# Five tiles' output stores move from ScalarE's queue to SP's, with a new written-out order for tiles 3 to 8

## The chip, the cores and the metric

The kernel runs on one core of one Trainium2 chip. The metric is the device time of one execution in microseconds (us), the median of several runs. The core has a matrix engine (TensorE, PE in the profile, with its weight loads listed as PEld), three engines for elementwise work (VectorE = DVE, ScalarE = ACT, GpSimd = POOL) and SyncE (SP), which does nothing here but start transfers. Each engine works through its own list of instructions in order and waits on semaphores where an instruction needs what another engine makes. A transfer is started by an instruction in the list of one engine (ACT, SP or POOL); "ACTq" and "SPq" in the profile are such starts.

## The reference

```python
q, k, v: [8 batches, 8 heads, 576, 64] float32
scores = (q @ k.T) / 8                  # per batch and head
scores = where(block_i >= block_j, scores, -1e9)   # blocks of 64 positions
attn   = softmax(scores) @ v
x      = attn.transpose(0, 2, 1, 3).reshape(4608, 512)
out    = (relu(x @ w_gate) * (x @ w_val)) @ w_out  # [512,1536], [512,1536], [1536,512]
```

`out` is [4608, 512] in float32.

## The kernel before

**Tiles.** The feed-forward part is worked in nine tiles of 512 rows of x. Tile j below 8 holds the first 512 positions of batch j; tile 8 holds the last 64 positions of all eight batches. While TensorE does the feed-forward of tile j, it also does the attention of batch j+1, and the inputs of batch j+2 are loaded. Tile 7 therefore carries no attention, and tile 8 none either.

**Order.** Nothing is left to a scheduler: from `with tc.manual_schedule` on, the instructions of all engines are issued in the order in which strings of tokens say. `ORDER_0` covers tiles 0 to 2. Tiles 3 to 6 all run `ORDER_3_6`, then come `ORDER_7` and `ORDER_8`; `program(j)` turns each token into instructions. As the order of the string is the order in every engine's list, moving a token moves its place on its own engine. `*n` after a token means n steps of it.

**The two matrix products of a tile.** Most pairs of 128 hidden features are made by a Strassen-like scheme with seven products in place of eight. For feature pair N the tokens are:
- `pN1` to `pN7`: the seven products, two steps each, and two matmuls of 128 x 256 columns into PSUM per step (`times`, L1363). They need sums of weights (`U..`, L979) and sums of x (`X4` to `X7`; `Y..` for tile 8; L1171).
- `pNa`, `pNu`, `pNw`: ScalarE copies a PSUM bank to an SBUF buffer (L1385). After that TensorE may write the bank again.
- `pNd`, `pNe`, `pNc`: VectorE adds a bank to such a buffer (L1389).
- `pNr`: relu on ScalarE (L1334); `pNH` and `pNL`: gate times value, giving half of a hidden tile hT (L1401, and L1405 with the relu included). `pNL` is on VectorE, `pNH` on VectorE or POOL.
- `gF`, `vF`, `rF`, `hF`: the same for one feature block without the scheme (L1339). Tiles 7 and 8 have none of these.

The product with w_out is done in the same way: `s....` are sums of hT (L1020), `M1` to `M7` the seven products, six steps of two matmuls each (L1061); `oa`, `ou`, `ow`, `oy` are ScalarE copies (L1106), `od`, `oe`, `oc` VectorE sums (L1100). In tile 8 `oy` is split into `oya` (ScalarE) and `oyb` (VectorE, L1118), `oc` into `oca` and `ocb`.

**Stores.** Each tile has four stores of 256 KB: `S2`, `S1`, `S0`, and the fourth, `S3`, which is put off into the next tile, where its token is `P`. They are issued in `put_block` (L893) for tiles 3 to 7: from ScalarE's queue, and for tile 2 from SP's. Tile 8's stores (`Sa`, `Sb`, `S2`, `Sya`, `S1`, `Syb`, two transfers each, L906) are spread over SP, ACT and POOL.

**Attention.** `Ai` makes the scores of head pair i of the next batch (L631), `Ei.` their exponentials on ScalarE (L636, L643), `Ci.` clears the masked corners (VectorE L1516 or POOL L1519), `Vi.` multiplies with v (L779), `Ni.` divides (L718), and `Ti` sends the result transposed into x by a transfer on SP (L862). `K` and `k` do the last 64 keys. `l0` to `l10` load q and k and `w0` to `w5` load v, started by POOL (L509); `d0` to `d3` transpose q and k by transfers on SP (L519 to L526).

**Where things go.** `ON_POOL` names the sums, products and clears that run on POOL, all others of their kind run on VectorE. `SLOTS` lists which of the rotating buffers each request takes (`sc` two and `ffnp` three PSUM buffers, `ob` five SBUF buffers of 128 x 512 float32, `gate_sb` three). `PAIR_BANK`, `OUT_BANK` and `AV_BANK` say which of the PSUM pools (`sc`, `one`, `ffn`) a product goes to.

Of the kernel before, what the change touches and what calls it, by code (L numbers as in the profile page):

```python
# [17 lines left out]
def kernel(  # L18
# [91 lines left out]
    ORDER_8 = """  # L110
        p01 p31 p01 p0a p17 p11*2 p1a X4 p07 p17 p07 p0w p06 p12 p06 p0u p12 p1c p16*2
        p04 p05*2 p0d p21 p1u p15*2 p31 p1w p1d p14*2 p1e p3a p04 p1L p0e p21 p2a p03*2
        p0r p0H p13 p02 p13 p1r p02 p0c P p1H p36 p26*2 p2u p27*2 p2w p41 p32 p25 p32
        p41 p4a p25 s0002 p0L s0102 p2d p3c p37*2 p3w p36 p3u p24*2 p2e p23*2 p2r p2H
        p34*2 p3e p35 p47 p35 p3d p22*2 p47 p2c p4w p3L p2L p42 p51*2 p5a p42 p33*2 p3r
        p3H p4c p46*2 p56 p44*2 p4u p4e p4L p56 p5u p57*2 p5w p45*2 p4d p55*2 p5d p54*2
        p5e M2 p52 p43 p52 p5c p5L p53 p43 p4r p4H p53 p5r p5H M1*2 M2 M1*4 M2*4 s0202
        s1002 s1202 oa s2002 s2202 M6*2 M7 s2102 M6*4 s1102 M7 s0302 s2302 M7*4 ou oca
        Sa M5*5 ocb s1302 Sb ow M5 od M4 S2 M4*3 M3*3 oya Sya M4*2 oe S1 M3*3 oyb Syb
# [38 lines left out]
        (7, 2): ('ffn', 'ffn', 'ffn'),
        (7, 3): ('one', 'ffn', 'sc'),
        (7, 4): ('ffn', 'one', 'ffn'),  # L160
        (7, 5): ('sc', 'sc', 'ffn'),
# [1655 lines left out]
```

## Time and profile before

| | |
|---|---|
| time, median of 3 runs | 344.81 us (344.55 to 344.91) |
| the profiled execution's own time | 344.71 us |
| its span | 342.8 us |
| mean granted TensorE clock | 0.997 |
| TensorE busy (matmuls) | 332.7 us, 97% |
| VectorE / ScalarE / POOL busy | 233.1 / 210.8 / 216.7 us |
| tile 3, tile 4, tile 5, tile 6 (start of one to start of the next) | 35.70, 35.62, 35.61, 34.83 us |
| tile 7; tile 8 to the end of the span | 28.00; 33.20 us |
| stores from ScalarE (L893 and earlier lines) | 28 transfers of 256 KB |

All times of instructions are from the profiled execution and count from the start of its span; times between runs are compared with the median. Copies, sums and products count as busy; starting a transfer does not, so ACTq and SPq rows stand apart from ACT's and SP's busy time. `[0.58 <-DVE hT L1405]` behind a row means that the engine was idle for 0.58 us before it and that an instruction of VectorE of line L1405 ended the wait. Matmuls are pipelined: a matmul of 256 columns starts 0.109 us after the one before when nothing is missing, though the row of one alone is longer.

### The profile page before, as it was taken

To read this page: it belongs to the slowest core of one execution; us is meant where nothing else is said; L and a number is where in the kernel's file an instruction comes from. 1 tells how busy PE (TensorE), PEld (TensorE's weight loads), DVE (VectorE), ACT (ScalarE), POOL (GpSimd) and SP (SyncE) were. 2 spreads that over 40 slices of the span, in tenths; PEclk is the share of its full clock that TensorE was granted. 3 is DMA by queue.
4 is the path that set the end of the run, shared out by engine and by line. 5 is a ranking of instruction groups with operands and counts; after the bars stand their busy time and mean duration, and the time that the engine had idled before them with its cause. 6 is when DMAs were issued, how large, how long until landed. Compare 5 with 4: busy or idle time off the path is not lost.

```text
span 342.8 us, 8917 instructions
## 1 busy us (share of the span) xinstructions
PE 332.7 (97%) x3477; PEld 233.8 (68%) x3518; DVE 233.1 (68%) x540; ACT 210.8 (61%) x344; POOL 216.7 (63%) x272
## 2 busy tenths in 40 slices
PE   8899999999999999999999999999999999999994
PEld 4544455545545558777877787777777788888883
DVE  4854445668637887389538972898279958966992
ACT  4942757588325882778558764876488727637731
POOL 2766566488695912787778967986514694750631
PEclk9999999999999999999999999999999999999998
DMA  8999999999998999799899989996510140002004
GB/s 242 294 351 371 368 230 238 240 163 155 187 197 137 144 158 137 165 143 121 111 165 120 130 116 153 128 137 118 138 33 2 33 122 12 2 31 94 33 0 122
DMA packets 155337, 50.06 MB, mean 146 GB/s; under 512 B 134496, under 2 KB 151648, under 8 KB 155296
## 3 DMA queue, kind: packets, MB, share of 16 engines
q0 software_dynamic: 70576, 9.12, 43.6%
q1 hardware_dynamic: 77536, 32.52, 43.0%
q10 hardware_dynamic: 7184, 7.87, 7.8%
q8 instruction: 27, 0.44, 0.5%
q14 instruction: 14, 0.11, 0.1%
HBM read 37.75 MB, written 9.44 MB: 138 GB/s over the span
## 4 chain that ended last, share of the span: by engine, by line
PE 88%; issue 4%; DVE 2%; ACT 2%; POOL 2%; POOLq 0%; DVEq 0%; ACTq 0%
PE ffnp L1179 16%; PE ffnp L1363 9%; PE ffnp L1339 8%; PE sc L1363 8%; PE sc L1061 6%; PE ffnp L1282 6%; PE ffnp L1061 6%; PE one L1363 5%; PE one L1061 4%; PE sc L631 3%; PE one L631 2%; PE one L779 2%; PE ffnp L779 2%; PE one L1179 2%; PE sc L779 1%
## 5 line engine op out<-in xcount | busy, mean ns | idle before, releaser
L636 ACT ACTIVATE attnT<-sc 128x1024 bf16<-128x1024 f32 x56 | 56.7, 1036 | 0.0
L1189 ACT ACTIVATE gate_sb<-ffnp 128x512 bf16<-128x512 f32 x35 | 20.6, 599 | 27.3 <-PE ffnp L1179 24.4
L1179 PE MATMUL ffnp<-xT,wg 128*128 128x512 bf16 x130 | 36.2, 379 | 0.6
L1061 PEld LDWEIGHTS <-stage 128*128 128x128 bf16 x336 | 32.0, 98 | 4.1 <-issue 0.2
L1363 PEld LDWEIGHTS <-stage 128*128 128x128 bf16 x288 | 27.3, 98 | 7.8
L779 PEld LDWEIGHTS <-attnT 128*128 128x128 bf16 x640 | 26.3, 98 | 7.7 <-DVE xnat L718 1.2
L1179 PE MATMUL ffnp<-xT,wv 128*128 128x512 bf16 x108 | 31.3, 380 | 0.2
L1199 DVE TENSOR_TENSOR hT<-gate_sb,ffnp 128x512 bf16<-128x512 bf16 x28 | 19.2, 684 | 14.9 <-PE ffnp L1179 12.0
L1389 DVE TENSOR_TENSOR ob<-ffnp,ob 128x512 f32<-128x512 f32 x29 | 19.8, 684 | 12.6 <-ACT ob L1385 12.6
L509 POOL DMA_DIRECT2D v_bf<-in_v_dram x30 | 24.3, 829 | 6.0 <-PE sc L793 3.1
L1061 PEld LDWEIGHTS <-hT 128*128 128x128 bf16 x252 | 24.2, 98 | 5.3 <-DVE hT L1405 1.1
L1363 PEld LDWEIGHTS <-wg 128*128 128x128 bf16 x224 | 21.9, 98 | 5.1
L1363 PEld LDWEIGHTS <-wv 128*128 128x128 bf16 x224 | 21.5, 98 | 5.3 <-ACT attnT L636 1.1
L1106 ACT COPY ob<-sc 128x512 f32<-128x512 f32 x13 | 7.6, 586 | 28.4 <-PE sc L1061 27.0
L1519 POOL MEMSET attnT<- 64x256 bf16 x34 | 10.2, 314 | 23.4 <-ACT attnT L636 16.0
L1282 PE MATMUL ffnp<-wo,hT 128*128 128x512 bf16 x91 | 23.1, 379 | 0.2
L1179 PEld LDWEIGHTS <-wg 128*128 128x128 bf16 x144 | 13.3, 98 | 13.8 <-issue 0.5
L1179 PEld LDWEIGHTS <-wv 128*128 128x128 bf16 x144 | 13.0, 98 | 14.3 <-issue 1.5
L1334 ACT ACTIVATE gate_sb<-ffnp 128x512 bf16<-128x512 f32 x30 | 17.6, 603 | 8.1 <-PE ffnp L1363 4.6
L509 POOL DMA_DIRECT2D q_bf<-in_q_dram x20 | 18.0, 908 | 5.0 <-DVE recip L752 4.0
L643 ACT ACTIVATE attnT<-one 128x512 bf16<-128x512 f32 (+1 forms) x28 | 15.0, 537 | 9.8 <-PE ffnp L631 8.4
L1020 POOL TENSOR_TENSOR stage<-hT,stage 128x512 bf16<-128x512 bf16 x15 | 17.4, 1167 | 4.2 <-DVE stage L1020 3.6
(228 smaller groups left out, 918.3 us busy)
## 6 DMA issues: line engine op xcount, KB each, us to landing
...
```

What stands on the lines that cost most here:

```text
L509: ins = nc.gpsimd.dma_start(dst, part_of)
L636: return lambda: nc.scalar.activation(at[:, :, lo : lo + 512], sc, AF.Exp, scale=scale)
L779: nc.tensor.matmul(av[:, p, :], at[:, col : col + 128], v_bf[b % 2][:, c, h, :], start=(p == 0), stop=(c == p), skip_group_check=True,)
L1061: nc.tensor.matmul(to, sums.of(c)[which][:, 128 * p : 128 * p + 128], right, start=first, stop=(c == 5), skip_group_check=True,)
L1179: nc.tensor.matmul(to, (wg, wv)[t][f // 4][:, c, 128 * (f % 4) : 128 * (f % 4) + 128], x[:, c], start=(c == 0), stop=(c == 3),)
L1189: nc.scalar.activation(gate_sb, gate, AF.Relu)
L1199: nc.vector.tensor_tensor(out=h, in0=gate_sb, in1=val, op=AX.mult)
L1282: nc.tensor.matmul(op, hT[f][:, 128 * s : 128 * (s + 1)], wo[f // 4][:, f % 4, n0:n1], start=(f == 0), stop=(f == 11),)
L1334: nc.scalar.activation(st[key], of, AF.Relu)
L1339: nc.tensor.matmul(to, (wg, wv)[t][f // 4][:, c, 128 * (f % 4) : 128 * (f % 4) + 128], x[:, c], start=(c == 0), stop=(c == 3),)
L1363: nc.tensor.matmul(st[key][:, 256 * k : 256 * k + 256], left[:, c, 128 * k : 128 * k + 128], right[:, c], start=new and (k, c) == (0, 0), ...
L1389: nc.vector.tensor_tensor(out=t, in0=st[n, of], in1=t, op=AX.add)
```

## The change

The stores of tiles 3 to 7 are issued from SP's queue, as those of tile 2 were. With that come new strings for tiles 3 to 6, 7 and 8, and new lists of buffers, banks and of what runs on POOL for them. The set of products, sums, copies and transfers is the same; `ORDER_0` is too. In the new order
- `P` is the first token of tiles 3 to 6 (before, some 5 us into the tile), the second of tile 7 (before, near its end), and in tile 8 it comes behind `S2`, near the end (before, early in the tile);
- the loads `l0` to `l8` and `w0`, `w1` come in the first third of tiles 3 to 6, `l0`, `l1` ahead of `X5`; `d0` comes with them; `T0` to `T3` come a little earlier;
- in tiles 3 to 6 `C00`, `C01`, `33H` and the like and `X4` go from POOL to VectorE; `X5`, `s0002` and `s1002` from VectorE to POOL. In tile 7 `X6` goes to VectorE, in tile 8 `81H` takes the place of `80H` on POOL; `U43` and `U45` go to POOL and `U46` to VectorE;
- in tile 7 and 8 the pairs and products come in another order; in tile 8 `ow` stands ahead of `Sb`, no longer behind it.

```diff
...
     ORDER_3_6 = """
-        l0 A0 E0t E0u g0*2 p12 w0 p12 X5 X7 E0s E0f X6 X4 K g0*2 g1*2 p11*2 p1a g1*2
-        p17*2 p16*2 C00 C01 p1c k V00 N00 P v1*2 p1u p15*2 p1w p1d p14 V01 N01 p14 p1e
-        p1L v1*2 r0 r1 p13*2 p1r v0*2 h1 A1 E1t v0*2 h0 p21*2 E1s p22*2 w1 p27*2 p2a
-        p26*2 E1u l1 w2 p31 p1H l2 l3 p2c p31 g8 U05 l4 p2w p24*2 w3 s0002 p2u p2e p2L
-        l5 l6 p25 g8 p25 p2d C11 p3a p36*2 p32 p37*2 E1f C10 V11 l7 N11 U06 l8 p3u p35
-        p3w p35 p3d g8*2 r8 p23*2 p2H l9 p34*2 p3e p33*2 p3r p32 A2 E2t E2u p3c p3L v8*4
-        h8 p57 p51*2 p57 p52 E2s V10 N10 p5a p56*2 p5w d0 d1 T1 p5u s0202 p3H p52 p5c g9
-        p54*2 p5e l10 s1102 g9*3 p55*2 p5d C21 p5L s1002 E2f r9 s0302 s1202 A3 E3t v9
-        E3f U45 s0102 p53*2 p5r C20 v9 V21 v9 N21 v9 M1 h9 V20 M1*2 p5H s2102 s2002 E3s
-        C30 N20 U47 M1*3 M7*2 T0 d2 d3 E3u C31 V30 M7 V31 N30 T2 oa N31 s2202 s2302 M6*6
-        ou M7*3 ow M2 M5*5 M4 M5 M4*3 od S2 M4*2 oe S1 M2 U46 U43 M3 U07 w4 s1302 M3*5
-        M2*4 oc oy S0 w5 T3 U03
+        P A0 E0t E0u g1*2 g0 l0 l1 K g0 X5 l2 g1*2 g0 p12 X7 X6 l3 d0 l4 l5 l6 E0s C01
+        p11*2 w0 E0f C00 w1 l7 p12 l8 X4 g0 p17*2 p1a p16*2 k V00 p1c N00 r0 w2 v1*2 d1
+        p1u p15*2 v1*2 p1w p14*2 p1d r1 h1 p1e V01 U05 N01 p13*2 p1r p1H v0*2 A1 E1t
+        v0*2 h0 E1s p21*2 p2a E1u C11 p22*2 p27*2 p1L s0002 p2c p2w p26*2 p2u p31*2 p3a
+        g8 p24*2 p2e p2L p32 p25*2 p36 p2d p36 p37 E1f C10 g8 p37 V11 N11 p3u g8 p35*2
+        p3w p3d p23 g8 p23 p2H r8 U06 l9 p34*2 p33*2 p3e p3r w3 l10 p32 A2 E2u U03 d2
+        s0102 p3c p3L v8*3 p3H v8 h8 s1002 p51 p57 p51 p52 p57 E2t E2s V10 N10 T1 T0 d3
+        p5a p52 p5c p56*2 g9*2 p5w p54*2 g9 p5u p5e g9 p55 E2f r9 p55 s1102 A3 E3t E3f
+        v9*3 p5d p5L s1202 p53*2 p5r v9 h9 C21 s0202 C20 V21 N21 U45 M1*2 w4 p5H s2002
+        E3s C30 E3u M1 V20 N20 T2 M1*3 oa M7*2 s2102 C31 M2 V30 N30 V31 N31 T3 s2202
+        s2302 U07 s0302 M6*6 ou M7 U46 U43 w5 M7 M2 M7*2 ow M5*4 M4 M5*2 od S2 M4*2 M2
+        M4*3 M2 U47 oe S1 s1302 M3*6 M2*2 oy S0 oc
     """
     ORDER_7 = """
-        p11 X5 X7 X6 X4 p01*2 p0a p02*2 p11 p1a p0c p12*2 p1c p06*2 p16*2 p07*2 p17*2
-        p0u p05*2 p21 p0w p1u p21 p04*2 p0d p0e p2a p15*2 p1w p1d p22 p03 p22 p03 p0r
-        p31 p14*2 p13*2 p1r p26 p31 p0L p27 p26 p27 p2c p1e p1H Y5 p1L p37*2 p0H s0002
-        s0202 s0102 p32*2 p2u p25 p3a p3c p36 p25 p36 p2w p24*2 p2d p2e p51*2 p3w p3u
-        p35*2 p3d p23*2 p2L p34*2 p5a p56 p33*2 p2r p2H p3e p3L p52 p57 p56 p41 p57 p41
-        p47 p3r p3H p52 p5c p42*2 p5u p55 p4a p4c p46*2 p47 p55 p5w p54 p5d p54 p5e M1
-        s1002 s1202 s1102 p4w p4u p44*2 p4e p45 p53 p45 p4d p53 M1 p5r P p4L p5L p5H
-        M2*2 M7 p43 M7 p43 p4r p4H s2002 s2202 s2302 M1*4 oa M2*4 M6*6 s2102 M7*4 ou
-        M5*3 ow M5*3 od S2 oc M4*6 s1302 s0302 oe M3*4 S1 Y7 Y6 M3*2 oy S0
+        X5 P p02 p32 p01*2 p0a p12 p11 p12 p11 X7 X6 X4 p07 Y5 p1a p1c p06*2 p0u p02 p0c
+        p07 p16*2 p05*2 p17 p0w p0d p17 p04*2 p0e p1u p15*2 p1w p14 p1d p14 p03*2 p0r
+        p0H p0L p1e p21*2 p2a p13 p22*2 p2c p32 p13 p1r p26 p31*2 p3a p26 p2u p1L p1H
+        s0102 s0002 s0202 p3c p27 p37 p51 p27 p2w p36*2 p37 p3u p25*2 p2d p24*2 p2e p35
+        p51 p35 p52 p3w p3d p23*2 p34 p5a p2r p2H p2L p34 p3e p52 p5c p33*2 p3r p3H
+        s1002 p57 p47 p56*2 p5u p3L s1102 p41*2 p4a p57 p5w p42*2 p55*2 p4c s1202 p5d
+        p47 p4w p46*2 p54*2 p5e p44*2 p4u p4e M1 p45*2 p4d p4L p5L p53*2 p5r p5H M2 M7*2
+        p43*2 p4r p4H s2002 s2202 s2302 M2 M1*5 oa M2*4 M6*6 s2102 M7*4 ou M5*2 s1302
+        M5*4 ow od S2 M4*6 oe S1 oc s0302 M3*6 oy Y7 Y6 S0
     """
     ORDER_8 = """
-        p01 p31 p01 p0a p17 p11*2 p1a X4 p07 p17 p07 p0w p06 p12 p06 p0u p12 p1c p16*2
-        p04 p05*2 p0d p21 p1u p15*2 p31 p1w p1d p14*2 p1e p3a p04 p1L p0e p21 p2a p03*2
-        p0r p0H p13 p02 p13 p1r p02 p0c P p1H p36 p26*2 p2u p27*2 p2w p41 p32 p25 p32
-        p41 p4a p25 s0002 p0L s0102 p2d p3c p37*2 p3w p36 p3u p24*2 p2e p23*2 p2r p2H
-        p34*2 p3e p35 p47 p35 p3d p22*2 p47 p2c p4w p3L p2L p42 p51*2 p5a p42 p33*2 p3r
-        p3H p4c p46*2 p56 p44*2 p4u p4e p4L p56 p5u p57*2 p5w p45*2 p4d p55*2 p5d p54*2
-        p5e M2 p52 p43 p52 p5c p5L p53 p43 p4r p4H p53 p5r p5H M1*2 M2 M1*4 M2*4 s0202
-        s1002 s1202 oa s2002 s2202 M6*2 M7 s2102 M6*4 s1102 M7 s0302 s2302 M7*4 ou oca
-        Sa M5*5 ocb s1302 Sb ow M5 od M4 S2 M4*3 M3*3 oya Sya M4*2 oe S1 M3*3 oyb Syb
+        p11 X4 p01 p12 p01 p0a p07*2 p0w p11 p1a p21*2 p06*2 p0u p12 p17 p1c p16*2 p17
+        p05*2 p0d p04 p1u p15*2 p1w p14 p1d p14 p1e p1L p2a p03*2 p0r p04 p0e p13*2 p1r
+        p31*2 p3a p02*2 p1H p0c p0L p27 p26*2 p36 p27 p32*2 p2u p25*2 p0H s0002 p2w p2d
+        p3c p37 p36 p37 p3w p41*2 p24*2 p2e p34 p23 p3u p34 p23 p2r p3e p35*2 p4a p3d
+        p22 p42 s0102 p22 p2c p2H p51*2 p5a p47*2 p4w p33 p46 p33 p3r p3H s1002 p46 p42
+        p4u p3L p44 p2L s1202 p4c p44 p4e p57 p56 p4L p45 p56 p5u p52*2 p5c p57 p5w p45
+        p55 M7 p4d M2 p55 p5d p54*2 p5e M1 p43*2 M1 p4r s0202 p5L p4H p53*2 p5r p5H M2
+        M1*4 oa M2*4 s2002 M6*2 s1102 M7 s2202 M6*4 ou s0302 s2102 s1302 oca Sa M7*4
+        M5*6 ocb ow Sb od S2 P M4*4 M3*2 s2302 M3 oya Sya M4*2 oe S1 M3*3 oyb Syb
...
     ON_POOL = set(
         """
-        33H 35H 3C00 3C01 3C10 3C11 3C20 3C21 3C30 3C31 3X4 3X6 3X7 3s0102
-        3s0202 3s0302 3s1302 3s2202 3s2302 43H 45H 4C00 4C01 4C10 4C11 4C20 4C21
-        4C30 4C31 4X4 4X6 4X7 4s0102 4s0202 4s0302 4s1302 4s2202 4s2302 53H 55H
-        5C00 5C01 5C10 5C11 5C20 5C21 5C30 5C31 5X4 5X6 5X7 5s0102 5s0202 5s0302
-        5s1302 5s2202 5s2302 63H 65H 6C00 6C01 6C10 6C11 6C20 6C21 6C30 6C31 6X4
-        6X6 6X7 6s0102 6s0202 6s0302 6s1302 6s2202 6s2302 70H 72H 7X4 7X5 7X6
-        7Y5 7Y7 7s0102 7s0202 7s0302 7s1002 7s1102 7s1202 7s1302 7s2302 80H 82H
-        83H 8s0002 8s0102 8s1002 8s1202 U03 U06 U07 U46
+        35H 3C10 3C11 3C20 3C21 3C30 3C31 3X5 3X6 3X7 3s0002 3s0102 3s0202
+        3s1002 3s1302 3s2202 3s2302 45H 4C10 4C11 4C20 4C21 4C30 4C31 4X5 4X6
+        4X7 4s0002 4s0102 4s0202 4s1002 4s1302 4s2202 4s2302 55H 5C10 5C11 5C20
+        5C21 5C30 5C31 5X5 5X6 5X7 5s0002 5s0102 5s0202 5s1002 5s1302 5s2202
+        5s2302 65H 6C10 6C11 6C20 6C21 6C30 6C31 6X5 6X6 6X7 6s0002 6s0102
+        6s0202 6s1002 6s1302 6s2202 6s2302 70H 72H 7X4 7X5 7Y5 7s0102 7s0202
+        7s0302 7s1002 7s1102 7s1202 7s1302 7s2302 81H 82H 83H 8s0002 8s0102
+        8s1002 8s1202 U03 U06 U07 U43 U45
         """.split()
     )
...
         rows = ob.rearrange("q (p n) -> q p n", n=256)
         if j < B:
             r0 = S * j + 256 * hi + 128 * p0
-            (nc.sync if j == 2 else nc.scalar).dma_start(
+            nc.sync.dma_start(
                 out[r0 : r0 + 128 * (p1 - p0), n].rearrange("(p q) n -> q p n", q=128),
                 rows,
             )
...
```

The lists of buffers (`SLOTS`) and of banks (`PAIR_BANK` for tiles 7 and 8, two entries of `OUT_BANK`, two of `AV_BANK`) are rewritten to go with the order.

More of the change, by code (lines that the diff above doesn't have):

```diff
@@ L46 @@
             "010101010101010010101010101010101010101010101010101010101001100011000101"
-            "1001100011000101100110001100010110011000110001011001011001000"
+            "10011000110001011001100011000101100110001100010110110110101"
         ),
@@ L50 @@
             "021021021020210210210210210210120210120202010101210120201201120120210211"
-            "201021102101020120120120121201202101202101202101210201201202120101212012"
-            "021021020102121010210201201202120101212012021021020102121010210202102010"
-            "2020201210"
+            "201021102101020120120120121201202101202101202101210220120120212010121020"
+            "122102102120210102012102201201202120101210201221021021202101020121020012"
+            "0120101212120102"
         ),
         "ob": (
-            "043210432104314021340123401321034120134021034013204103214013210341201340"
-            "210340134013204230214302"
+            "043210432104314024130421301421043012043120143104201304213014210430120431"
+            "201431042310432403423042"
         ),
         "gate_sb": (
-            "021021021021021021021021021021021021021201201210210212012012102102120120"
+            "021021021021021021021021021021021021021210120101210212101201012102102102"
             "1201"
@@ L155 @@
         (6, 5): ('ffn', 'one', 'ffn'),
-        (7, 0): ('ffn', 'one', 'one'),
+        (7, 0): ('one', 'ffn', 'ffn'),
         (7, 1): ('sc', 'sc', 'sc'),
[L158 to L161, printed above, removed]
+        (7, 2): ('ffn', 'sc', 'ffn'),
+        (7, 3): ('one', 'ffn', 'ffn'),
+        (7, 4): ('ffn', 'sc', 'one'),
+        (7, 5): ('sc', 'ffn', 'ffn'),
         (8, 0): ('one', 'sc', 'ffn'),
-        (8, 1): ('ffn', 'ffn', 'sc'),
-        (8, 2): ('sc', 'one', 'sc'),
+        (8, 1): ('ffn', 'ffn', 'ffn'),
+        (8, 2): ('sc', 'one', 'ffn'),
         (8, 3): ('ffn', 'ffn', 'ffn'),
         (8, 4): ('sc', 'ffn', 'one'),
-        (8, 5): ('ffn', 'ffn', 'sc'),
+        (8, 5): ('sc', 'ffn', 'ffn'),
     }
@@ L170 @@
         """
-        33H 35H 3C00 3C01 3C10 3C11 3C20 3C21 3C30 3C31 3X4 3X6 3X7 3s0102
-        3s0202 3s0302 3s1302 3s2202 3s2302 43H 45H 4C00 4C01 4C10 4C11 4C20 4C21
-        4C30 4C31 4X4 4X6 4X7 4s0102 4s0202 4s0302 4s1302 4s2202 4s2302 53H 55H
-        5C00 5C01 5C10 5C11 5C20 5C21 5C30 5C31 5X4 5X6 5X7 5s0102 5s0202 5s0302
-        5s1302 5s2202 5s2302 63H 65H 6C00 6C01 6C10 6C11 6C20 6C21 6C30 6C31 6X4
-        6X6 6X7 6s0102 6s0202 6s0302 6s1302 6s2202 6s2302 70H 72H 7X4 7X5 7X6
-        7Y5 7Y7 7s0102 7s0202 7s0302 7s1002 7s1102 7s1202 7s1302 7s2302 80H 82H
-        83H 8s0002 8s0102 8s1002 8s1202 U03 U06 U07 U46
+        35H 3C10 3C11 3C20 3C21 3C30 3C31 3X5 3X6 3X7 3s0002 3s0102 3s0202
[6 more added lines that the diff above has]
+        8s1002 8s1202 U03 U06 U07 U43 U45
         """.split()
     )
-    OUT_BANK = {(2, 'v'): 'ffn', (2, 'w'): 'ffn', (2, 'x'): 'one', (3, 'v'): 'one', (3, 'w'): 'sc', (3, 'x'): 'ffn', (4, 'v'): 'one', (4, 'w'): 'sc', (4, 'x'): 'ffn', (5, 'v'): 'one', (5, 'w'): 'sc', (5, 'x'): 'ffn', (6, 'v'): 'one', (6, 'w'): 'sc', (6, 'x'): 'ffn', (7, 'v'): 'one', (7, 'w'): 'ffn', (7, 'x'): 'ffn', (8, 'v'): 'sc', (8, 'w'): 'ffn', (8, 'x'): 'one'}
+    OUT_BANK = {(2, 'v'): 'ffn', (2, 'w'): 'ffn', (2, 'x'): 'one', (3, 'v'): 'one', (3, 'w'): 'sc', (3, 'x'): 'ffn', (4, 'v'): 'one', (4, 'w'): 'sc', (4, 'x'): 'ffn', (5, 'v'): 'one', (5, 'w'): 'sc', (5, 'x'): 'ffn', (6, 'v'): 'one', (6, 'w'): 'sc', (6, 'x'): 'ffn', (7, 'v'): 'one', (7, 'w'): 'ffn', (7, 'x'): 'sc', (8, 'v'): 'one', (8, 'w'): 'ffn', (8, 'x'): 'one'}
     UP_MEM = {
@@ L189 @@
     }
-    AV_BANK = {0: ('one', 'one'), 1: ('sc', 'sc'), 2: ('ffn', 'one'), 3: ('ffn', 'sc')}
+    AV_BANK = {0: ('one', 'ffn'), 1: ('sc', 'sc'), 2: ('ffn', 'one'), 3: ('sc', 'ffn')}
     LAST_CHUNKS = {}
```

## The prediction, made before the changed kernel was run

> **What bounds the kernel now.** I read the page first, then the busy times in seven stretches (one for each tile 3 to 7, two for tile 8), then tiles 7 and 8 in order of time, then the store's line.
>
> ```profile
> span 342.8 us, 8917 instructions
> PE 332.7 (97%) x3477; PEld 233.8 (68%) x3518; DVE 233.1 (68%) x540; ACT 210.8 (61%) x344; POOL 216.7 (63%) x272
> ```
>
> TensorE works for 332.7 of 342.8 us; the other engines have a third of their time free. In the stretches (columns: length, busy time of each engine with its instructions, granted clock, DMA share, GB/s) tiles 4 and 5 are full, and the holes lie in tiles 7 and 8:
>
> ```profile
> 175.54:211.16 35.62, 35.36 (x413) 27.44 (x418) 24.96 (x57) 24.56 (x41) 28.59 (x36) 1.00 1.30 132
> 211.16:246.77 35.61, 35.35 (x412) 27.43 (x418) 24.94 (x57) 24.55 (x41) 26.83 (x34) 1.00 1.16 136
> 281.60:309.60 28.00, 27.77 (x255) 24.51 (x253) 22.82 (x39) 15.13 (x27) 16.03 (x14) 1.00 0.09 30
> 309.60:336.00 26.40, 25.75 (x234) 22.44 (x232) 21.23 (x39) 15.62 (x28) 8.87 (x7) 1.00 0.14 41
> 336.00:342.80 6.80, 2.45 (x21) 1.80 (x19) 1.30 (x3) 0.37 (x1) 1.27 (x2) 0.85 0.44 116
> ```
>
> The change keeps every matmul, so it can win only what TensorE waits now. Going by the distance from one matmul's start to the next (0.109 us for 256 columns when nothing is missing), tiles 3 to 6 wait nowhere for as much as 0.1 us. The waits are these. Tile 7, 0.40 us: the third step of product M1 waits for p5L on VectorE.
>
> ```profile
> 300.30 1.28 DVE L1405 SCALAR_TENSOR_TENSOR hT<-ob,k_bf 128x512 bf16<-128x512 f32 x2
> 301.64 0.94 PE L1061 MATMUL ffnp<-wo,hT 128*128 128x256 bf16 x7 [0.23 <-DVE hT L1405]
> ```
>
> Tile 8, 0.14 us at 325.93 (p5w stands behind another copy on ScalarE) and 0.47 us before 329.38, again M1 behind p5L:
>
> ```profile
> 328.63 0.69 DVE L1405 SCALAR_TENSOR_TENSOR hT<-ob,k_bf 128x512 bf16<-128x512 f32 x1
> 329.38 0.39 PE L1061 MATMUL ffnp<-wo,hT 128*128 128x256 bf16 x2 [0.31 <-DVE hT L1405]
> ```
>
> Then 0.51 us, because the copy ow stands behind the issue of stores Sa and Sb on ScalarE:
>
> ```profile
> 333.36 1.47 ACTq L906 DMA_DIRECT2D out_dram<-ob  x2
> 334.87 0.59 ACT L1106 COPY ob<-sc 128x512 f32<-128x512 f32 x1 [1.49 <-DVE stage L1020]
> 335.51 0.71 PE L1061 MATMUL sc<-stage,hT 128*128 128x256 bf16 x5 [0.35 <-ACT ob L1106]
> ```
>
> and 0.19 us, M3's second half behind the copy oya. Behind the last matmul come the last stores:
>
> ```profile
> 336.21 3.45 SPq L906 DMA_DIRECT2D out_dram<-ob  x4
> 337.23 0.37 ACT L1118 COPY ob<-ffnp 128x256 f32<-128x256 f32 x1 [1.78 <-PE ffnp L1061]
> 337.66 0.82 PE L1061 MATMUL ffnp<-wo,stage 128*128 128x256 bf16 x6
> ```
>
> So there is 0.40 + 0.14 + 0.47 + 0.51 + 0.19 = 1.71 us to be had, and 2.5% of clock nowhere.
>
> **The stores.** The store's line has both queues already:
>
> ```profile
> L893 ACTq DMA_DIRECT2D out_dram<-ob x20: 378/378/390, 172.1 to 316.4; - x20
> L893 SPq DMA_DIRECT2D out_dram<-ob x4: 390/435/1255, 138.5 to 140.7; - x4
> DMA to landing us min/median/max: 2.1/2.7/6.0
> ```
>
> 20 issues of 0.378 us leave ScalarE: 7.56 us, 1.5 in a tile. In tiles 3 to 6 they lie beside idle time there; tile 5 issues the first of its four at 214.03, and ScalarE stands idle 3.79 us before a copy near its end:
>
> ```profile
> 214.03 0.38 ACTq L893 DMA_DIRECT2D out_dram<-ob  x1
> 245.17 0.59 ACT L1106 COPY ob<-sc 128x512 f32<-128x512 f32 x1 [3.79 <-PE sc L1061]
> ```
>
> I take 0 for the gain; bounds -0.38 (one issue ahead of a copy on the path, once) and 0. On SP each costs 0.39 to 1.26 us, four to a tile, at most 5.0 us. SP issues nine transposes in tile 4 (qTm 3.15, kTm 3.12, four xT 5.55 together, qTt 1.20, kTt 1.21, xTt 1.20: 15.4 us of 35.6), so 20.5 of 35.6 us at worst. The stores now follow T3 and precede d0, which waits for loads until about 7.4 us into the next tile; nothing is queued behind them that is due earlier. What a late store could hold up is its ob buffer. By the sums of the new order S2, S1, S0 and P issue at 33.2, 34.5, 35.9 and 36.9 us of their tile, and their buffers are next written at 40.2, 40.7, 45.4 and 46.4. With the longest landing of 6.0 us that leaves 1.0 us at the nearest, with the median 2.7 us over 4. Cost 0; bounds 0 and 4 x 0.3 us (a 6 us landing behind a 1.26 us issue).
>
> **Tiles 3 to 6, the order and the engines.** Durations are rows: ACT copy 0.59 us (the next result 0.49 later), VectorE f32 sum 0.69, bf16 sum on VectorE 0.42, on POOL 1.16, 0.27 from a matmul's start to its result, 0.05 to 0.06 to hand it on. VectorE gives up s0002, s1002 and X5 (3 x 0.42) and takes X4 (0.42), C00 and C01 (2 x 0.165) and 33H (0.69): +0.18 us a tile on 24.9 of 35.6. POOL gives up 33H (1.16), two memsets (2 x 0.31) and X4, and takes X5 and two sums (2 x 1.16): +0.5 on about 28. Neither becomes the bound. Between a product and the matmul that overwrites or needs it, the new order leaves the same least distances as the old: 0.87 us of matmuls over an ACT copy (needed: 0.27 + 0.59), 1.07 over a VectorE sum (0.27 + 0.04 + 0.69 + 0.06 = 1.06). One place is tighter: A3 takes its bank from p5e after 0.97 us, so about 0.09 us may be lost, or nothing if p5e finds VectorE free early. POOL now issues l0, l1 (0.88 us each) before X5 and l2 before X7 and X6; X7 ends some 1.8 and X6 3.0 us into the tile, p17 wants it at 3.6 and p16 at 4.0: covered by 1.0 us or more. That cover falls if T3 lands late: X7 waits for it. The other loads, T0 to T2, x_sums, U43 to U47 and the bank choices start sooner or as late, with work of microseconds behind them: 0. Together +0.1 us over four tiles; bounds 0 and 4 x 0.09 = +0.36 in this case.
>
> **Tile 7.** P moves to the second token, X6 to VectorE, the products into another order. Only M1 counts: it now starts after p45 and p5L is queued on VectorE behind p5e and p4d. The third step of M1 comes 1.97 us after p45 by matmuls alone, p5L ends at 2.21 + 0.06: a wait of 0.30, and 0.03 at M2. The same sum gives 0.40 for the old order, as measured. Gain 0.40 - 0.33 = 0.07 us; ends: 0.40 gained if p4d is early, 0.28 lost if one more bf16 sum (0.34) stands ahead.
>
> **Tile 8.** The wait at 325.93 goes: p5u now follows p56 at once, over 0.87 us: -0.14. At M1, from the end of p54: p5e to 1.06, s0202 in between on the same engine, p5L 1.31 to 2.00, wanted at 1.53: 0.53 with the hand-over, +0.06. ow now stands ahead of Sb's issue, so it starts after M7 with M5 (six steps, 1.31 us) as cover: -0.51; next late is od, 0.87 us before M3: a wait of 0.08. oya is unchanged: 0.19. So 0.80 in place of 1.31: a gain of 0.51, between 0.1 (ow delayed by Sa alone, 0.58 us) and 1.04 (no M1 wait).
>
> P, 256 KB, which in the old order went out early in this tile on ScalarE, now goes out on SP after S2 and ahead of Sya, S1 and Syb. Syb is issued at 339.10 now, and its landing 2.65 us later, with about 1 us behind it, sets the end. S2 is issued at 336.21, Sya at 337.63: room for 0.55 us of P after S2's 0.64 and the 0.2 gained. P's row is 0.39 to 1.26 us, median 0.435: mostly hidden; bounds 0 and +0.35. I take +0.1, nearer the median.
>
> The row shows only issue time, not what P's 272 packets do to Syb in the DMA engines; at 46 ns a packet over 16 engines they are 0.78 us of transfer. The Trainium skill, "DMA: Bandwidth & Descriptors", section "Queues, rings and completion order", says that each queue has a ring of its own on every engine; its section "Two DMAs through the same engine are not ordered" says that within one queue descriptors start in order. By that rule P's packets stand ahead of Syb's and would add up to 0.78 us to the end; the trace shows no large store ahead of small ones on SP at the end, so it neither agrees nor disagrees.
>
> **The sum.** The profiled execution took 344.71 us (span 342.8, 1.9 around it), 0.10 under the median of 344.81. 344.71 - 0.07 - 0.51 + 0.1 + 0.1 = 344.33. I forecast 344.3 us, 0.15% under the median, inside the 0.2% (0.69 us: 344.12 to 345.50) that a measurement of this kernel can tell from no change.
>
> **The rivals.**
> 1. Faster: the M1 waits of tiles 7 and 8 go too, because p4d and s0202 find VectorE free early. For it: VectorE is only 80% busy there. Against it: p5e and p5L are one chain whose length I took from rows. 344.33 - 0.33 - 0.3 = 343.7; some of it, 344.0.
> 2. Slower: a tile of 3 to 6 loses, four times. The place is VectorE before p5e. The least margin over a VectorE sum was 0.01 to 0.03 us and is nil here now, so each delay on VectorE ahead of it, say s0102 or 33H placed one earlier than its input is ready, goes straight to TensorE. One bf16 sum is 0.34 us: 4 x 0.34 = +1.36, 345.7; one f32 sum 0.60: 346.7. It decides from 0.3 us a tile. For it: no slack, and T3 to X7 to p17 is a second place of the kind. Against it: my queue sums show the inputs ready.
> 3. P in front of Syb at the end delays the last landing by its packets: 0.78 in place of 0.1, 345.0. For it: one ring. Against it: P has about 2.5 us before Syb is issued.
> 4. The change moves nothing, since no store lay on the path and the M1 waits stay: 344.7.
>
> **How the numbers follow.** Forecast 0.40 (its own range 344.1 to 344.7), rival 1 0.20, rival 2 0.25, rivals 3 and 4 0.15. Faster by over 0.2%: rival 1 and 0.06 of the forecast, 0.26. Slower: rival 2 and a piece of rival 3, 0.27. Within: 0.47. The range runs from 343.8, most of rival 1, to 346.0, the nearer half of rival 2; 0.17 is left out.
>
> **What would show it.** In the profile after: stores of tiles 3 to 7 under SPq with 0.39 to 0.5 us each; stretches of tiles 3 to 6 of 35.6 to 35.7 us; M1's wait of about 0.3 us in tile 7 and 0.5 in tile 8; ow right after M7, no wait at M4; the last Syb landing within 0.3 us of where it stands to the last matmul now. I am wrong if a tile of 3 to 6 grows by 0.3 us, with a VectorE sum, X7 or an ob buffer as releaser, or if the end behind the last matmul grows by more than 0.35 us.

## The result and the profile after

The changed kernel takes 346.38 us (median of 5 runs, 345.63 to 347.03) where the kernel before takes 344.81: a ratio of 1.0044, 95% interval 1.0031 to 1.0058. It is slower, by 0.4%, and 0.38 us beyond the range that was forecast. Run a second time, on another chip, it took 345.95 us beside 344.98 (1.0028, 1.0017 to 1.0039), so about 1 us of the loss came in both series and the rest varies.

The page of the changed kernel still shows a bound TensorE; 41 more matmul records came through than before, so TensorE's two sums cannot be compared.

```profile
span 343.5 us, 8971 instructions
PE 335.4 (98%) x3518; PEld 233.7 (68%) x3518; DVE 240.8 (70%) x549; ACT 210.3 (61%) x344; POOL 213.4 (62%) x263
```

To compare stage by stage I cut both spans at the start of the last matmul of each tile's output product. The stretches of the changed kernel (tiles 3, 4, 6, 7, 8, and from the last matmul to the end; columns as in the prediction):

```profile
138.62:174.66 36.04, 35.93 (x418) 27.36 (x416) 26.60 (x57) 24.44 (x41) 29.02 (x36) 1.00 1.29 132
174.66:210.38 35.72, 35.72 (x418) 27.54 (x416) 27.25 (x58) 24.51 (x41) 28.20 (x35) 1.00 1.30 131
...
246.10:281.81 35.71, 35.71 (x418) 27.55 (x416) 27.62 (x61) 24.50 (x41) 18.01 (x20) 1.00 0.17 47
281.81:309.56 27.75, 27.74 (x254) 24.40 (x252) 21.97 (x38) 15.45 (x28) 14.31 (x12) 1.00 0.11 37
309.56:338.05 28.49, 28.10 (x255) 24.43 (x252) 23.14 (x43) 15.80 (x29) 9.20 (x8) 1.00 0.12 34
338.05:343.50 5.45, 0.27 (x3) 0.00 (x0) 0.59 (x2) 0.00 (x0) 0.62 (x1) 0.96 0.59 175
```

and of the kernel before, cut in the same way:

```profile
138.80:174.50 35.70, 35.44 (x413) 27.36 (x416) 23.95 (x55) 24.95 (x41) 29.77 (x37) 1.00 1.20 134
174.50:210.12 35.62, 35.36 (x413) 27.44 (x416) 24.95 (x56) 24.56 (x41) 28.59 (x36) 1.00 1.30 130
...
281.35:309.34 27.99, 27.76 (x254) 24.50 (x252) 22.60 (x38) 15.16 (x28) 16.24 (x14) 1.00 0.10 32
309.34:338.20 28.86, 28.18 (x254) 24.47 (x252) 22.16 (x41) 15.99 (x29) 9.52 (x8) 1.00 0.15 43
338.20:342.85 4.65, 0.27 (x3) 0.00 (x0) 0.59 (x2) 0.00 (x0) 0.61 (x1) 0.78 0.51 144
```

| stretch | before | after | difference |
|---|---|---|---|
| start to tile 3 (same order in both) | 138.80 | 138.62 | -0.18 |
| tile 3 | 35.70 | 36.04 | +0.34 |
| tiles 4 to 6, each | 35.62 | 35.72 | +0.10 |
| tile 7 | 27.99 | 27.75 | -0.24 |
| tile 8 | 28.86 | 28.49 | -0.37 |
| last matmul to the end | 4.65 | 5.45 | +0.81 |

The differences are taken before rounding, and with tiles 4 to 6 counted three times they add up to 0.66 us, the difference of the spans (342.85 and 343.50). The last matmul starts 0.15 us earlier than before, thanks to 0.18 us at the start, where the code is the same. This execution took 345.63 us, the least of the five runs.

The waits that the change was to shorten are where the prediction's sums put them: by the distance from one matmul's start to the next, M1 behind p5L waits 0.17 us in tile 7 (forecast 0.30) and 0.53 in tile 8 (forecast 0.53), and ow's wait is gone.

```profile
301.12 0.69 DVE L1405 SCALAR_TENSOR_TENSOR hT<-ob,k_bf 128x512 bf16<-128x512 f32 x1
301.86 0.33 PEld L1061 LDWEIGHTS <-hT 128*128 128x128 bf16 x4 [0.28 <-DVE hT L1405]
...
329.07 0.68 DVE L1405 SCALAR_TENSOR_TENSOR hT<-ob,k_bf 128x512 bf16<-128x512 f32 x1
329.81 0.61 PE L1061 MATMUL ffnp<-wo,hT 128*128 128x256 bf16 x4 [0.36 <-DVE hT L1405]
```

At the end P is issued at 336.89, Sya, S1 and Syb from 337.57 on, Syb at 339.05, which is 0.05 us earlier than before. Only the landings are late:

```profile
336.21 0.64 SPq L906 DMA_DIRECT2D out_dram<-ob  x1
336.89 0.59 SPq L893 DMA_DIRECT2D out_dram<-ob  x1
337.57 2.04 SPq L906 DMA_DIRECT2D out_dram<-ob  x3
```

The store's line over the stretch behind P, one queue at a time, gives the time from issue to landing. SP's last three and ScalarE's last two in the changed kernel:

```profile
L906 SPq DMA_DIRECT2D out_dram<-ob x3: 508/567/718, 337.6 to 339.1; - x3
DMA to landing us min/median/max: 3.3/3.3/4.0
...
L906 ACTq DMA_DIRECT2D out_dram<-ob x2: 473/480/488, 337.5 to 338.9; - x2
DMA to landing us min/median/max: 3.1/3.1/3.2
```

and in the kernel before:

```profile
L906 SPq DMA_DIRECT2D out_dram<-ob x3: 474/555/621, 337.6 to 339.1; - x3
DMA to landing us min/median/max: 1.9/2.6/2.6
...
L906 ACTq DMA_DIRECT2D out_dram<-ob x2: 497/502/507, 337.6 to 339.0; - x2
DMA to landing us min/median/max: 2.2/2.4/2.5
```

The issues take about the same time as before; each of these transfers needs 0.6 us or more longer to land, and so does POOL's last one (3.3 us in place of 2.7). All of them share the core's 16 DMA engines. Over the 3.75 us that begin 0.5 us ahead of the last matmul, these engines' busy share (the last figure but one) is 0.76 before and 0.95 in the changed kernel: with P there, nearly no gap is left.

```profile
337.70:341.45 3.75, 0.77 (x6) 0.44 (x5) 1.09 (x2) 0.00 (x0) 0.61 (x1) 0.91 0.76 200
...
337.55:341.30 3.75, 0.77 (x6) 0.44 (x5) 1.09 (x2) 0.00 (x0) 0.62 (x1) 1.00 0.95 270
```

### The profile page after: what moved, and what is told of

Read it like the earlier page. It is cut to its first block, busy times and chain, and to the rows that moved or that the text cites. A ratio compares the mean times of both kernels' runs of the same rounds, so it can differ in the third digit from the quotient of the medians.

```text
span 343.5 us, 8971 instructions
## 1 busy us (share of the span) xinstructions
PE 335.4 (98%) x3518; PEld 233.7 (68%) x3518; DVE 240.8 (70%) x549; ACT 210.3 (61%) x344; POOL 213.4 (62%) x263
## 4 chain that ended last, share of the span: by engine, by line
PE 90%; issue 3%; ACT 2%; POOL 2%; DVE 2%; POOLq 0%
PE ffnp L1179 16%; PE ffnp L1363 10%; PE ffnp L1339 9%; PE sc L1363 8%; PE sc L1061 6%; PE ffnp L1282 6%; PE ffnp L1061 5%; PE one L1363 5%; PE one L1061 4%; PE sc L631 4%; PE one L631 2%; PE ffnp L779 2%; PE one L1179 2%; ACT attnT L595 2%; PE one L779 2%
## 5 line engine op out<-in xcount | busy, mean ns | idle before, releaser
L1179 PE MATMUL ffnp<-xT,wg 128*128 128x512 bf16 x140 | 37.9, 379 | 0.0
L1189 ACT ACTIVATE gate_sb<-ffnp 128x512 bf16<-128x512 f32 x35 | 20.5, 598 | 27.1 <-PE ffnp L1179 26.9
L1179 PE MATMUL ffnp<-xT,wv 128*128 128x512 bf16 x112 | 32.1, 380 | 0.0
L1020 POOL TENSOR_TENSOR stage<-hT 128x512 bf16<-128x512 bf16 x18 | 21.7, 1211 | 11.6 <-DVE hT L1401 8.8
L1519 POOL MEMSET attnT<- 64x256 bf16 x26 | 7.7, 306 | 29.3 <-ACT attnT L636 13.3
L1389 DVE TENSOR_TENSOR ob<-ffnp,ob 128x512 f32<-128x512 f32 x33 | 22.5, 683 | 1.9 <-PE ffnp L1363 1.6
L1334 ACT ACTIVATE gate_sb<-ffnp 128x512 bf16<-128x512 f32 x28 | 16.9, 605 | 7.7 <-PE ffnp L1339 4.3
L1363 PE MATMUL sc<-perm,wv 128*128 128x256 bf16 x128 | 20.4, 273 | 0.0
```

The costliest lines, as they stand in the source:

```text
L1020: (eng or nc.vector).tensor_tensor(out=of(part), in0=a, in1=b, op=op)
L1179: nc.tensor.matmul(to, (wg, wv)[t][f // 4][:, c, 128 * (f % 4) : 128 * (f % 4) + 128], x[:, c], start=(c == 0), stop=(c == 3),)
L1189: nc.scalar.activation(gate_sb, gate, AF.Relu)
L1363: nc.tensor.matmul(st[key][:, 256 * k : 256 * k + 256], left[:, c, 128 * k : 128 * k + 128], right[:, c], start=new and (k, c) == (0, 0), ...
L1389: nc.vector.tensor_tensor(out=t, in0=st[n, of], in1=t, op=AX.add)
```

## The experiments

Four theories stand behind the expectations. A: P at the end costs the 0.8 us. B: stores on SP's queue delay something in tiles 3 to 7. C: the new order of tiles 3 to 6 has lost its slack. D, formed after the first runs: tile 3 waits by chance for a store of tile 2. The kernels of one series ran on one chip beside the kernel before, and each is compared with that.

**P early in tile 8.** One token of the changed kernel is moved.

```diff
-        p31*2 p3a p02*2 p1H p0c p0L ...
+        p31*2 p3a p02*2 P p1H p0c p0L ...
-        M5*6 ocb ow Sb od S2 P M4*4 ...
+        M5*6 ocb ow Sb od S2 M4*4 ...
```

> The changed kernel with one token moved: in tile 8 the store P goes out early (before p1H) and no longer behind S2. Theory A, the end: P's 272 packets stand ahead of Syb's in SP's queue, which is the 0.80 us by which the stretch from the last matmul's start to the end of the span grew (5.45 against 4.65). Then this kernel ends 4.6 to 4.7 us behind its last matmul and takes 346.4 - 0.8 = 345.6 us. Theory B, the loss lies in tiles 3 to 7 alone: the stretch stays near 5.4 and the time at 346.4.

Measured: 345.26 us beside 344.95 (1.001, 0.9985 to 1.0034). From the last matmul (341.59) to the end (346.2) the profile has 4.6 us again, and the last stores land in 2.2 to 2.7 us. Theory A stands. The profiled execution itself was a long one (348.35 us), of use for the rest: it lost 2.5 us before tile 3, where the code is the same in all kernels, and tile 3 took 37.08 us, with this:

```profile
147.99 0.59 ACT L1385 COPY ob<-sc 128x512 f32<-128x512 f32 x1 [1.37 <-DMA out_dram<-ob]
148.63 0.60 PE L1363 MATMUL sc<-perm,wv 128*128 128x256 bf16 x4 [0.88 <-ACT ob L1385]
```

The copy p1w waits for a store and TensorE behind it; the tile is 1.04 us longer than in the changed kernel. Its buffer is that of tile 2's S0, issued 0.9 us into tile 3, which landed 5.9 us later. In the changed kernel's own profile the same store landed after 4.0 us and no wait followed. So a loss of up to 1 us by chance is possible there: theory D.

**Stores back on ScalarE.**

```diff
-            nc.sync.dma_start(
+            (nc.sync if j == 2 else nc.scalar).dma_start(
```

> The changed kernel with the stores of tiles 3 to 7 back on ScalarE's queue, all orders as changed. Theory B, stores on SP's queue delay transposes or stores in tiles 3 to 7 in a way that varies from run to run: the time falls by the 0.75 us by which the median lies over the profiled run, to 345.6 us, and the spread of 1.4 us shrinks to 0.4. Theory C, the new order of tiles 3 to 6 has no slack over VectorE and loses 0.1 us a tile and more by chance: unchanged in tiles 3 to 6, 35.7 us each. At the end P is now in ScalarE's queue ahead of Sya's and Syb's first halves; if the queue alone decides, the end is late by up to 0.8 us as well.

Measured: 347.44 us beside 344.95 (1.0079, 1.0049 to 1.011), and 36.43 us in each of tiles 4 to 6. The fall that theory B forecast did not come: with the new order SP's queue is worth 0.71 us a tile over ScalarE's. A small cost of SP's own would be hidden in that difference. On ScalarE, P as a tile's first token waits for the sum oc, and the exponentials E0t and E0u stand behind it; then K waits for them:

```profile
175.32 0.93 ACTq L893 DMA_DIRECT2D out_dram<-ob  x2
176.30 0.60 ACT L643 ACTIVATE attnT<-one 128x512 bf16<-128x512 f32 x1 [1.01 <-PE sc L631]
176.95 0.28 PE L660 MATMUL one<-qTt,kTt 128*128 128x64 bf16 x4 [0.32 <-ACT attnT L643]
```

The end of this run tells more. It took 4.66 us, as before, although P stands in ScalarE's queue ahead of the halves of Sya and Syb. ScalarE reached P at 337.34, 3.1 us ahead of the last matmul, where SP had it 1.2 us ahead in the changed kernel. P's packets moved between 338.4 and 339.4 us; in the changed kernel the DMA engines stand idle in that place (336.05 to 337.05, share 0.00). All stores from S2 on landed in 2.1 to 2.7 us, S2 among them, issued 1.2 us behind P while P was still in flight. So a large store ahead of small ones costs nothing where the DMA engines have room for it.

```profile
337.34 0.62 ACTq L893 DMA_DIRECT2D out_dram<-ob  x1
...
338.43:339.43 1.00, 1.00 (x10) 0.76 (x9) 0.46 (x2) 0.00 (x0) 0.58 (x1) 1.00 0.77 262
339.93:343.68 3.75, 0.77 (x6) 0.44 (x5) 1.08 (x2) 0.00 (x0) 0.62 (x1) 1.00 0.78 208
```

**The queue alone, in the old order.** The same line, the other way, in the kernel before.

> The kernel before with nothing but the queue changed: stores of tiles 3 to 7 on SP. In its order T3 stands behind S2, S1 and S0 in SP's list, and S0 waits for the tile's last copy. So T3 is issued some 0.7 us into the next tile in place of 5 us before its start, lands about 4.5 us into it, and g0, which reads all of xT, wants it at about 1.3: some 3 us lost at the start of tiles 4 to 7, 345 + 12 = 357 us. If the queue is harmless whatever the order: 344.8.

Measured: 363.05 us (two runs, 1.0508), tiles 4 to 7 at 40.36, 41.74, 38.07 and 30.67 us: 16.0 us more than before, where 12 were expected. (3.0 us more lie ahead of tile 3, where nothing was changed.) The mechanism is the one expected, larger by a third; the list of waits shows who waited for the transposes:

```profile
POOL perm L1171 <- DMA xT<-xnat: 13.6, 2, 7.0
...
PE ffnp L1363 <- DMA xT<-xnat: 8.0, 3, 3.6
```

Queue and order thus belong together: each alone loses much more than the 0.10 us that they lose together in each of tiles 4 to 6.

**Old tiles 3 to 6, new tiles 7 and 8.** `ORDER_3_6` with its lists and ScalarE's queue as before, `ORDER_7` and `ORDER_8` as changed, P early in tile 8.

> Tiles 3 to 6 as in the kernel before (order, engines, stores on ScalarE), tiles 7 and 8 as changed (stores of tile 7 on SP), with P early in tile 8. Theory C with A: tiles 7 and 8 keep their gains of 0.24 and 0.37 us, the end is as before, tiles 3 to 6 take 35.62 us again: 344.8 - 0.6 = 344.2 us. If the gains of tiles 7 and 8 belong to chance: 344.8.

Measured: 345.01 us (1.0002, 0.9981 to 1.0022), not 344.2. Tile 8 took 28.49 us as expected, tile 7 took 28.47. Its first product stood 0.73 us, because at this joint, which neither kernel has, it takes the PSUM buffer that oc of tile 6 still reads:

```profile
281.75 0.69 DVE L1045 TENSOR_TENSOR ob<-ffnp,ob 128x512 f32<-128x512 f32 x1 [1.36 <-PE ffnp L1006]
282.49 0.38 PE L1308 MATMUL ffnp<-xT,wg 128*128 128x256 bf16 x2 [0.56 <-DVE ob L1045]
```

**The changed kernel again,** unaltered, beside the next three.

> The changed kernel as it is, so that it stands beside the next three on one chip. Theory A (P at the end costs 0.8 us) and theory D (in tile 3 the copy p1w waits by chance for the store S0 of tile 2, which lands 4 to 6 us after its issue because the loads now start with the tile): 346.0 to 346.6 us, end stretch 5.4 us behind the last matmul, stores of tile 2 issued from 139.5 us on landing after 4.0 us and more, tiles 4 to 6 35.72 us each as before. If the 346.38 was of that chip alone: 345.3.

Measured: 345.95 us (345.82 to 346.27) beside 344.98. Tiles 3 to 8 repeat the first profile to 0.01 us (36.04, 35.72, 35.72, 35.72, 27.75, 28.49), and the end took 5.3. S0's store landed after 4.7 us; the copy p1w waited 0.23 us for it, and TensorE lost nothing by that. What repeats is therefore tile 3, tiles 4 to 6 and the end.

**Loads later in tile 3 alone.** As the first experiment, with l0 to l8, w0 to w2, d0 and d1 behind p1w.

> The changed kernel with P early in tile 8, and in tile 3 alone the loads l0 to l8, w0 to w2 and d0, d1 moved behind p1w (from about 5 us into the tile on). Theory D: the three stores of tile 2 that are issued about 1 us into tile 3 land in 3.4 to 3.7 us again, p1w waits for none of them, and the median falls from 345.26 to 344.9 us with fewer runs above 346. If the late landings are not the loads' doing: they stay at 4 to 6 us and the median stays at 345.3.

Measured: 350.03 us (1.0154), much slower, so it says nothing by its time. The part that was asked is in its profile. Nothing on POOL held the loads back until p1w, so they began at 140.39 us, 1.2 us into the tile. The stores issued at 140.07 and 140.51 landed in 3.3 and 3.8 us, about as in the kernel before (3.4 to 3.7) and below the 4.0 to 6.2 of the new order; the third, issued at 141.02 with the loads under way, took 5.6. That speaks for theory D, without being the test that was meant. The loss is one that I made: with the loads bunched, the clear C10 came late on POOL and a product with v waited for it.

```profile
154.45 1.78 POOL L523 DMA_DIRECT2D k_bf<-in_k_dram  x2
156.27 0.31 POOL L1533 MEMSET attnT<- 64x256 bf16 x1
156.63 0.73 PE L793 MATMUL sc<-v_bf,attnT 128*128 128x65 bf16 x10 [3.22 <-POOL attnT L1533]
```

**The joint mended.** As the fourth experiment, with the names of the three `ffnp` buffers in tiles 7 and 8 exchanged.

> Tiles 3 to 6 as before, tiles 7 and 8 as changed, P early in tile 8, and the three ffnp buffers of tiles 7 and 8 renamed so that p02 and p32 at the start of tile 7 do not take the bank that the sum oc of tile 6 still reads (in the run before this cost 0.73 us at 281.65). Expected if that wait was a thing of the joint only: tile 7 in 27.75 us, tile 8 in 28.49, the end in 4.6, 344.9 - 0.7 = 344.2 us. Otherwise 345.0 again.

Measured: 344.53 us beside 344.98 (0.9986, 0.9977 to 0.9994), a little faster than both kernels; tile 7 in 27.82 us, tile 8 in 28.48, 4.6 at the end. The gains of the new tiles 7 and 8 are real.

**s0202 behind p5L.**

```diff
-        ... p5e M1 p43*2 M1 p4r s0202 p5L p4H p53*2 ...
+        ... p5e M1 p43*2 M1 p4r p5L s0202 p4H p53*2 ...
```

> The same, with s0202 behind p5L on VectorE in tile 8 in place of ahead of it. p5L starts right behind p5e (1.06 in place of 1.31 us after p54), so the wait of M1's third step falls from 0.53 to about 0.28 us: 344.0 us. If s0202 is then late for M2: no gain, 344.2.

Measured: 344.52 us (0.9985, 0.9976 to 0.9993). M1's wait fell from 0.53 to 0.32 us, and two waits of 0.25 and 0.11 appeared for the sums behind it; tile 8 took 28.61. The place s0202 had was as good.

**Twelve instructions more on VectorE.** In the four profiles above in which the new order of tile 3 is unaltered, tile 3 has one wait of 0.28 us that the other tiles have not: p33 waits for p3d, and p3d starts late. In the changed kernel:

```profile
153.42 0.60 PE L1363 MATMUL ffnp<-perm,stage 128*128 128x256 bf16 x4
...
154.48 0.69 DVE L1389 TENSOR_TENSOR ob<-ffnp,ob 128x512 f32<-128x512 f32 x1 [0.30 <-PE ffnp L1339]
...
155.23 0.60 PE L1363 MATMUL ffnp<-xT,stage 128*128 128x256 bf16 x4
```

p3d starts 1.06 us after the product that it reads began; in tile 4 it starts 0.71 us after it (190.13 and 189.42). The matmul named as releaser is not one that p3d reads.

```diff
     nc.vector.memset(zeros[:, 128:512], 0.0)
+    for i in range(12):
+        nc.vector.memset(zeros[:, 128 + 16 * i : 144 + 16 * i], 0.0)
```

> The changed kernel with P early in tile 8 and twelve small memsets more on VectorE at the very start, which fill columns that are zero already. In tile 3 p3d starts 0.35 us late on VectorE although all it waits for is there (TensorE then waits 0.28), in every run of the new order and in no other tile. If that belongs to the place of the instruction in VectorE's stream, the gap moves to an instruction twelve places earlier and tile 3 takes about 35.8 us; if it belongs to the work of tile 3, it stays at p3d and tile 3 at 36.04. Nothing else should change; the start may be 0.5 us longer.

Measured: tile 3 in 35.76 us (344.71 us for the one run). The same three instructions:

```profile
153.97 0.60 PE L1365 MATMUL ffnp<-perm,stage 128*128 128x256 bf16 x4
...
154.68 0.69 DVE L1391 TENSOR_TENSOR ob<-ffnp,ob 128x512 f32<-128x512 f32 x1
...
155.50 0.60 PE L1365 MATMUL ffnp<-xT,stage 128*128 128x256 bf16 x4
```

p3d starts 0.71 us after its product and TensorE does not wait. So the gap hangs on where the instruction stands in VectorE's stream, not on the work of tile 3. It did not show at the instruction twelve places earlier; what makes it is open. One thing in the trace moves with it: of two 8 KB DMA packets of the kind `instruction` that start at 155.90 us in the changed kernel, one starts at 148.84 with the twelve memsets, the other at 155.70. That they have to do with the gap is not shown; in the first experiment they come 5 us behind p3d.

**The 0.10 us of a tile.** Two small waits were seen in each of tiles 4 to 6, 0.05 at A3 and 0.05 at V10. One step of v9 goes ahead of A3, C10 goes to VectorE, and the list of `ffnp` buffers is rewritten to go with that.

> The changed kernel with P early in tile 8 and two edits in tiles 3 to 6: one step of v9 goes ahead of A3 (0.22 us more between p5e's matmuls and A3, which takes its bank), and the clear C10 goes from POOL (0.31 us) to VectorE (0.165). Theory C: the 0.10 us that a tile lost are 0.05 at A3 and 0.05 at V10, whose weights wait for C10; tiles 4 to 6 then take 35.62 us as in the kernel before, and the time is 0.4 us under that of the same kernel without the two edits, about 344.9. If one of the two is not a cause, 35.67 us.

Measured: 352.04 us (1.0202). Both edits fail for reasons of order. C10 on VectorE waits for its exponential with all of VectorE's list behind it, and v9 a step earlier needs a buffer that the relu on ScalarE has not left:

```profile
154.74 0.48 PE L760 MATMUL sc<-v_bf,attnT 128*128 128x65 bf16 x10 [1.59 <-DVE attnT L1497]
...
201.57 0.38 PE L1320 MATMUL ffnp<-xT,wv 128*128 128x512 bf16 x1 [0.35 <-ACT gate_sb L1315]
```

That the two waits are what a tile loses is thus read from the profile of the changed kernel alone; no run took them away.

**P late, from ScalarE's queue.**

```diff
-        M5*6 ocb ow Sb od S2 P M4*4 M3*2 s2302 M3 oya Sya ...
+        M5*6 ocb ow Sb od S2 M4*4 M3*2 s2302 M3 oya P Sya ...
```

> The changed kernel with P at the end as late as there, but issued from ScalarE's queue, behind oya and ahead of Sya's half. If packets of one queue stand behind those ahead of them, only ScalarE's later stores land late and the four of SP in 2.2 to 2.7 us, so the end stretch is set by ScalarE's half of Syb, some 5.2 us. If it is the shared DMA engines, the stores of SP and POOL that are issued after P land late too, by 0.6 us and more, and the stretch is 5.3 us or more whichever queue P is in.

Measured: 346.24 us in its one run, and 5.2 us from the last matmul (338.96) to the end. That is the first reading's figure (some 5.2) and just under the second's (5.3 or more); the landings decide. SP's last three stores, in whose queue P no longer is:

```profile
L906 SPq DMA_DIRECT2D out_dram<-ob x3: 475/566/622, 338.4 to 339.9; - x3
DMA to landing us min/median/max: 3.0/3.1/3.7
```

They land 0.2 to 0.3 us sooner than with P in their own queue, and still 0.5 to 1.1 us later than in the kernel before. POOL's lands after 3.1 us in place of 2.7, ScalarE's after 3.0 and 3.1 in place of 2.2 and 2.5. So the delay is not one of P's own queue, and the DMA engines are as full as in the changed kernel (share 0.97 over the same 3.75 us):

```profile
338.46:342.21 3.75, 0.77 (x6) 0.44 (x5) 1.09 (x2) 0.00 (x0) 0.62 (x1) 0.91 0.97 272
```

The Trainium skill says the same ("DMA: Bandwidth & Descriptors", section "Issuing engines are not separate DMA queues": transfers started by different engines run on the same 16 DMA engines and interleave), and the order within one queue, which the prediction weighed from that page, can account for the 0.2 to 0.3 us at most.

The same profile has theory D a second time. S0 of tile 2 landed 6.1 us into tile 3, p1w waited for it, and tile 3 took 36.41 us, 0.37 more than the 36.04 without a loss:

```profile
145.37 0.59 ACT L1385 COPY ob<-sc 128x512 f32<-128x512 f32 x1 [0.70 <-DMA out_dram<-ob]
```

**Two parts undone, timed.** P early and the twelve memsets, as in the experiment on VectorE.

> The kernel with P early in tile 8 and the twelve memsets, now timed, to see whether the parts found so far close the sum. Against the kernel before, from the profiles: tiles 3 to 6 +0.06 + 0.10 + 0.10 + 0.10, tile 7 -0.24, tile 8 -0.37, the end 0, the start 0: -0.25 us, so 344.7 us where the kernel before takes 344.95, with single runs up to 1 us higher where p1w waits for S0's store in tile 3. If the loss of the median has another cause that is in no profile: 345.3 us or more.

Measured: 344.51 us beside 344.88 (0.999, 0.9975 to 1.0005). Its stretches are 35.76, 35.72, 35.72, 35.72, 27.75 and 28.48 us and 4.7 at the end. The same orders and queue that lost 0.97 us lose nothing with these two parts undone. One run of eleven took 346.57, as one in fifteen of the kernel before did.

## Why the prediction was wrong, by its own steps

**The end of tile 8** is the step that failed. The prediction took issue time as P's price ("mostly hidden; bounds 0 and +0.35. I take +0.1"). Issue time was hidden, Syb was even issued 0.05 us earlier; the price is in the transfers, and the end grew by 0.81 us (0.66 in the second profile). The 0.78 us, worked out from P's packets, stood there as a rival with P's head start against it ("P has about 2.5 us before Syb is issued"). The rival had the size right and the reason too narrow: P delays stores of every queue, not those behind it in its own, because its packets fall into the stretch in which the shared DMA engines already carry the last stores. A head start of 2.2 us did not help; P issued 1.9 us sooner, where the engines are idle, cost nothing ("Stores back on ScalarE").

**Tile 3** has a term that the sum lacked, 0.28 us by the place of p3d in VectorE's stream. No row of the trace of before gives it. With it tile 3 grew by 0.34 us with a VectorE sum as releaser, which is a sign of being wrong that the prediction named, though not for the reason it gave. **Tile 3's stores** failed as a step too: the cover of "1.0 us at the nearest" was worked out for the stores that tiles 3 to 6 issue, but tile 3 waits for those of tile 2, which the unchanged order issues 0.9 to 1.9 us into tile 3. S0 has to land by about 5.7 us into the tile: landing at 6.1 cost 0.37 us and landing at 6.8 cost 1.04. It landed at 5.0, 5.6, 6.1 and 6.8 in four profiles, at 4.5 to 5.4 in the others of this order, and at 4.3 in the kernel before; that the loads now run beside it is the likely reason. This can explain single runs up to 1 us over the others; that it made the first five runs 0.4 us longer than the later six was not shown. The cover itself was reckoned wrongly: by its own figures S1's buffer (34.5 and 40.7) leaves 0.2 us after a landing of 6.0, not 1.0. In the changed kernel's profile no copy or sum waited for it, as the stores of tiles 3 to 7 landed in 4.1 us or less.

**Tiles 4 to 6**: "+0.1 us over four tiles; bounds 0 and 4 x 0.09 = +0.36" was 0.10 a tile. The place named, A3 after p5e, waited 0.05 us where 0.09 was the bound; the other 0.05 us, V10 behind C10, I had costed at nothing. The slower rival (0.34 us in each of four tiles) did not come about. VectorE's work was misjudged, at no cost in time: it grew from 24.95 to 27.25 us in tile 4, not by 0.18. The account of the change leaves out s0302, which also goes from POOL to VectorE in tiles 3 to 6, and two of VectorE's bf16 sums there, s2102 and s0302, take 1.06 and 2.48 us beside sums on POOL, where every such sum on VectorE took 0.42 in tile 4 before. The longer one, with the sum on POOL beside it:

```profile
204.85 2.48 DVE L1020 TENSOR_TENSOR stage<-hT,stage 128x512 bf16<-128x512 bf16 x1
205.18 1.17 POOL L1020 TENSOR_TENSOR stage<-hT,stage 128x512 bf16<-128x512 bf16 x1
```

TensorE waited for neither; why they take longer was not tested.

**Tiles 7 and 8** were right in mechanism: a gain of 0.07 + 0.51 = 0.58 was forecast, 0.24 + 0.37 = 0.61 came. That the total fits is partly luck, as tile 7 gained 0.17 us more and tile 8 0.14 less than forecast. M1 in tile 8 fits to 0.01 us; in tile 7 its wait was 0.17, not 0.30, as p5L was done earlier than my chain of sums had it; M3's wait behind od was 0.14 in place of 0.08, and one of 0.06 came at p56. **The stores' queue** was taken as worth 0, which the old rows supported. With the new order SP's queue is worth 0.71 us a tile over ScalarE's; with the old order it costs 2.5 to 6.1 us a tile.

Put together: 344.71 - 0.18 + 0.34 + 0.30 - 0.24 - 0.37 + 0.81 = 345.37, and 0.26 us more outside the span (2.13 in place of 1.87) make the profiled execution's 345.63. It lies 1.30 us over the 344.33 of the prediction's sum: 0.71 by P, 0.34 by tile 3, 0.20 by tiles 4 to 6 and 0.26 outside the span, less 0.18 at the start and 0.03 in tiles 7 and 8. The median of the first five runs is another 0.75 us higher, and the cause of that part stays open.
